# Attention outputs transposed by VectorE in 32x32 blocks, row maxima transposed in a score bank, and LN1 scaled on GpSimd

## The chip, the cores and the metric

The kernel runs on one core of a Trainium2 chip. A core has TensorE (PE, matrix products and transposes into PSUM), VectorE (DVE), ScalarE (ACT), GpSimd (POOL) and SyncE (SP, which issues the DMAs here). The metric is device time in microseconds (us) of one execution; several executions are timed and the median is taken. A trace of one execution shows what each engine did and what each wait ended on.

## The reference

One transformer block with adaptive layer norm: 2048 rows of width 448, 16 heads of width 28, a causal window of 256, and an MLP of width 1792 with the Mish activation.

```python
sa, ca, ga, sb, cb, gb = (silu(c) @ w_mod).reshape(1, 6, 1, -1)[:, i]   # i = 0..5
h = layernorm(x) * (1 + ca) + sa
q, k, v = (h @ wqkv) split into 16 heads of 28
scores = q @ k.T * 28 ** -0.5, masked to 0 <= i - j < 256
x = x + ga * ((softmax(scores) @ v) @ wo)
h = layernorm(x) * (1 + cb) + sb
x = x + gb * (mish(h @ w1 + b1) @ w2)
```

All inputs and the output are float32.

## The kernel before

**Precision.** A float32 product is built from a rounded high part (`float32r`) and the remainder: hi x hi, hi x lo and lo x hi are accumulated in PSUM. `wo` has 448 = 3 x 128 + 64 rows; in the last chunk the 64 rows and their remainders are stacked on 128 partitions, so it takes two products instead of three and an output tile takes 11 products.

**Stages.** The rows are worked in four groups of 512 (`NG`). Per group come LN1 (`gen_ln1`), the transpose of its rows (`gen_hT`), the q, k and v products (`gen_qkv`), the attention of 16 heads, the output product with `wo` (`gen_oT`, `gen_wo`), and LN2. The MLP (`f1_mm`, `ff2`) follows for all groups. The attention of group g is one software pipeline over all 64 heads; the work of the neighbouring groups fills the gaps.

**The pipeline.** A head has three steps; step u = 3s + k belongs to head s and part k. In a step PE does in this order: the product of an earlier step's probability remainders with v (`PV(u-3, Pl)`), the scores of this step (`B`), the scores of a head three ahead for the row maxima (`A`), filler products, one more `A`, and the product of earlier probabilities with v (`PV(u-2, Ph)`). ACT takes the exponential twice (`P` in float32, `Ph` rounded), POOL subtracts them (`Pl`, in `SP(u)`), DVE adds the mask to the scores of `A` and takes the row maximum (`junk`, `mx`). `M2` turns the maxima of two heads with one PE transpose; DVE splits the result into two parts (`mr`) and a DMA writes them into two extra rows of q, so that the scores of `B` come out with the maximum subtracted.

**The attention output.** `PV` accumulates a head in one PSUM bank `pv` as 60 rows: 28 rows from the high part of v, row 28 the sum of the probabilities, three zero rows, and 28 rows from the remainder of v. `EV` copies it to SBUF (ACT; DVE for the last three heads), two heads to a tile `O2`. `E` turns the two heads with four PE transposes of 124 columns into the bank `tr`; `E2` (ACT) copies the remainder rows out of it, `E3` takes the reciprocal of the sums and adds the two parts (DVE) and scales (POOL) into `on`. When the 16 heads of a group are done, `gen_oT` turns `on` back with 16 PE transposes, and ACT and DVE split it into high part and remainder for `wo`.

**What sets the order.** Every engine works its own instructions in program order, which the loop writes out by hand. Filler work for PE is paid out by a credit per step (`RATE`), side work on the other engines by `side_step`, and DMAs that are not urgent from the list `later`. PSUM has eight banks: `sA` 2, `sB` 2, `mm` 2, `tr` 1, `pv` 1. A tile that is allocated again waits until the readers of the older one are done.

Of the kernel before, what the change touches and what calls it, by code (L numbers as in the profile page):

```python
# [51 lines left out]
def adaln_block(ctx: ExitStack, tc: tile.TileContext, x, wqkv, wo, w1, b1, w2, c, w_mod, out):  # L52
# [104 lines left out]
    mask = kq.tile([128, 384], F32, name="mask")  # L157
# [67 lines left out]
    def gen_ln(tiles, pl, xn_tiles, key, mv=None):  # L225
# [12 lines left out]
        for t in range(4):  # L238
            xn = xs[t]
            DVE.tensor_scalar(xn[:, 0:D], tiles[t], mv[:, t, 0:1], rs[:, t:t + 1],  # L240
                              op0=ALU.subtract, op1=ALU.mult)
            if t:
                dup(xs[t - 1])
            yield xs
# [66 lines left out]
    def tile_mms(p, ps):  # L311
        m = 0
        for n, (a, b) in enumerate(ps):
            PE.matmul(p, b, a, start=(n == 0), stop=(n == 10))  # L314
# [185 lines left out]
    first_tiles([(0, bank("pv", 1, "qk0_0")), (3, bank("tr", 1, "qk0_3"))])  # L500
# [17 lines left out]
    O2 = []  # L518
    for i in range(2):
        t = att.tile([128, GT], F32, name=f"o2_{i}")  # L520
        POOL.memset(t[32:64, :], 0.0)
        O2.append(t)
    wo3 = [mid.tile([128, D], F32R, name=f"wo3_{i}", tag="wo", bufs=7) for i in range(4)]
    wol = [mid.tile([128, D], F32R, name=f"wol_{i}", tag="wo", bufs=7) for i in range(3)]
# [5 lines left out]
    def stg(pl, name):  # L530
        return pl.tile([128, 512], F32, name=name, tag="stg", bufs=4)
# [19 lines left out]
    def gen_mod_wo():  # L551
# [14 lines left out]
        for ci in range(4):  # L566
# [5 lines left out]
            split_lo(w, wo3[ci], wol[min(ci, 2)], ci, DVE)  # L572
# [40 lines left out]
    def gen_oT(g, tag, bufs, oT_pool):  # L613
        o = on[g]
        oh, ol = OT[g] = new_T(f"o{g}", oT_pool)

        def oT_out(p, ci):
            DVE.tensor_tensor(ol[:, ci], p, oh[:, ci].bitcast(F32), op=ALU.subtract)

        for ci in range(4):  # L620
            p = bank(tag, bufs, f"ot{g}{ci}")
            tr_chunk([o[:, t] for t in range(4)], ci, p)
            ACT.activation(oh[:, ci], p, AF.Copy)
            pipe.add(1, lambda p=p, ci=ci: oT_out(p, ci))
# [3 lines left out]
            if g == NG - 1:  # L628
                yield
# [6 lines left out]
    def gen_wo(g, tag, bufs):  # L636
# [14 lines left out]
        for t in range(4):  # L651
# [16 lines left out]
    mx, Pt, Ph, Pl, pvb, et, olt = {}, {}, {}, {}, {}, {}, {}  # L668
    junk = att.tile([128, 384], F32, name="junk")

    def A(i, t):
# [5 lines left out]
        p = bank("sA", 2, f"sA{i}_{t}")  # L677
        PE.matmul(p[:, c0:384], q[0:84, t * 128:(t + 1) * 128], k[0:84, t * 128 + c0:t * 128 + 384],  # L678
# [5 lines left out]
    def M2(pr):  # L684
        p = bank("tr", 1, f"mt{pr}")
# [57 lines left out]
    def EV(i):  # L743
        o = O2[i // 2 % 2][64 * (i % 2):64 * (i % 2) + 60]
        if i < NS - 3:
            ACT.activation(o, pvb[i][0:60, :], AF.Copy)  # L746
        else:
            DVE.tensor_copy(o, pvb[i][0:60, :])  # L748

    def E(pr):  # L750
        g, h = divmod(2 * pr, H)
        p = bank("tr", 1, f"et{pr}")
        for t in range(4):
            PE.transpose(p[:, t * 128:t * 128 + 124], O2[pr % 2][0:124, t * 128:(t + 1) * 128], ident[0:124, 0:124])  # L754
        et[pr] = p.rearrange("p (t a d) -> p t a d", t=4, a=2)

    def E2(pr):
        olt[pr] = att.tile([128, 4, 2, 28], F32, name=f"ol{pr}", tag="ol", bufs=2)
        ACT.activation(olt[pr], et[pr][:, :, :, 32:60], AF.Copy)
# [420 lines left out]
```

## Time and profile before

| what | value |
|---|---|
| three runs, median (lowest to highest) | 718.11 us (716.7 to 719.73) |
| profiled execution | 719.96 us |
| span from its first to its last instruction | 718.2 us |
| mean granted TensorE clock | 0.99 |
| attention pipeline | about 50 to 420 us of the span |
| MLP | about 420 us to the end |

The span is cut out of the profiled execution, which has 1.8 us around it. An engine's busy time is the union of its instructions; on PE, products overlap one another, so the distance between starts tells what one costs when PE is full, and not its duration.

### The profile page before, as it was taken

The page shows a single profiled execution, that of the slowest core. Times are in us where ns is not written, and L with a number is a line of the kernel's source. Part 1 is how long each engine was busy: PE and PEld are TensorE (multiplying, and loading weights), DVE is VectorE, ACT ScalarE, POOL GpSimd, SP SyncE. Part 2 cuts the span into 40 slices and gives each one's busy share as a digit, 9 for nine tenths or more (in the row PEclk, how much of TensorE's full clock was granted, in tenths as well). Part 3 has the DMA queues.
Part 4 walks back from the last instruction along what each step waited for, and adds up shares of the span by engine and source line. Part 5 has one row for each costly group of instructions (what it writes and reads, how often), then busy time and mean ns, then how long its engine had stood idle before and what let it go on. Part 6 is the DMA issues. An engine that isn't in the chain of part 4 may idle for free.

```text
span 718.2 us, 12057 instructions
## 1 busy us (share of the span) xinstructions
PE 694.9 (97%) x4049; PEld 597.3 (83%) x4049; DVE 380.0 (53%) x1018; ACT 390.9 (54%) x740; POOL 327.0 (46%) x358
## 2 busy tenths in 40 slices
PE   8999999999999999999999899999999999999996
PEld 8777878788898888898887688888888888888885
DVE  5688657788555878656768642434323232322112
ACT  4538778768766768767868774243224222422221
POOL 6636778676666767666869744422010000000002
PEclk9999999999999999999999899999999999999999
DMA  7865763453761653744672165400200020001001
GB/s 215 257 211 178 251 204 122 148 158 125 212 207 50 203 166 88 230 137 137 216 223 75 52 216 157 116 1 2 102 1 1 4 99 1 0 7 45 0 1 51
DMA packets 48249, 83.86 MB, mean 117 GB/s; under 512 B 6142, under 2 KB 26348, under 8 KB 48188
## 3 DMA queue, kind: packets, MB, share of 16 engines
q1 hardware_dynamic: 47724, 83.10, 37.1%
q8 instruction: 32, 0.52, 0.3%
q14 instruction: 29, 0.24, 0.1%
q10 hardware_dynamic: 464, 0.00, 0.0%
HBM read 53.45 MB, written 29.36 MB: 115 GB/s over the span
## 4 chain that ended last, share of the span: by engine, by line
PE 72%; issue 11%; DVE 8%; DMA 4%; ACT 2%; POOL 1%; SPq 1%; POOLq 0%; DVEq 0%; ACTq 0%
PE z L915 15%; PE pv L740 9%; PE qk L314 8%; PE sA L678 5%; PE acc L1098 5%; PE acc L1100 5%; PE acc L1099 5%; PE sB L708 5%; PE wo L314 4%; PE qk_v L314 4%; PE sB L719 3%; DVE junk L680 3%; PE et L754 2%; DMA q<-mr 1%; DMA scr<-st 1%
## 5 line engine op out<-in xcount | busy, mean ns | idle before, releaser
L730 POOL TENSOR_TENSOR Pl<-P,Ph 128x512 fp32r<-128x512 f32 (+2 forms) x192 | 234.5, 1229 | 87.1 <-ACT Ph L723 49.4
L680 DVE CUSTOM_DVE_ANT_0 junk<-sA,mask 128x384 f32<-128x384 f32 (+2 forms) x256 | 135.2, 528 | 97.8 <-PE sA L678 89.5
L722 ACT ACTIVATE P<-sB 128x512 f32<-128x512 f32 (+2 forms) x192 | 109.8, 572 | 66.9 <-PE sB L719 61.7
L923 DVE TENSOR_TENSOR al<-t,ah 128x512 fp32r<-128x512 f32 x56 | 38.7, 692 | 199.7 <-ACT ah L922 199.7
L921 ACT ACTIVATE t<-z,b1c 128x512 f32<-128x512 f32 x56 | 38.5, 688 | 188.8 <-PE z L915 181.6
L723 ACT ACTIVATE Ph<-sB 128x512 fp32r<-128x512 f32 (+2 forms) x192 | 109.2, 569 | 0.0
L678 PE MATMUL sA<-k,q 84*128 84x384 f32 (+2 forms) x256 | 100.9, 396 | 2.2 <-DVE mx L680 1.5
L915 PE MATMUL z<-hhf,w 128*128 128x512 f32 x224 | 89.6, 400 | 0.0
L915 PE MATMUL z<-hlf,w 128*128 128x512 f32 x224 | 88.4, 395 | 0.0
L1098 PE MATMUL acc<-w2h,ah 128*128 128x448 f32 x224 | 82.0, 366 | 0.0
L1100 PE MATMUL acc<-w2h,al 128*128 128x448 f32 x224 | 81.7, 365 | 0.0
L1099 PE MATMUL acc<-w2l,ah 128*128 128x448 f32 x224 | 81.4, 364 | 0.0
L740 PE MATMUL pv<-Ph,v 128*60 128x256 f32 (+2 forms) x352 | 77.6, 295 | 3.6 <-DVE o L748 2.3
L740 PE MATMUL pv<-Pl,v 128*60 128x256 f32 (+2 forms) x352 | 74.4, 286 | 2.3 <-POOL Pl L730 2.3
L708 PE MATMUL sB<-q,k 86*128 86x256 f32 (+1 forms) x352 | 74.7, 286 | 1.4 <-DMA q<-mr 1.4
L915 PE MATMUL z<-hhf,w1l 128*128 128x512 f32 x168 | 66.3, 395 | 0.0
L708 PEld LDWEIGHTS sB<-q,k 86*128 86x128 f32 x352 | 62.4, 191 | 2.9 <-issue 1.2
L740 PEld LDWEIGHTS pv<-Ph,v 128*60 128x60 f32 x352 | 46.0, 135 | 18.0 <-ACT o L746 3.2
L719 PE MATMUL sB<-fdmask,identr 128*128 128x128 bf16 (+1 forms) x320 | 60.6, 255 | 0.0
L678 PEld LDWEIGHTS sA<-k,q 84*128 84x128 f32 x256 | 48.9, 192 | 8.5 <-DVE mx L680 5.9
L740 PEld LDWEIGHTS pv<-Pl,v 128*60 128x60 f32 x352 | 45.7, 133 | 11.0 <-POOL Pl L730 3.9
L1107 POOL TENSOR_TENSOR yo<-yo,x 128x448 f32<-128x448 f32 (+1 forms) x4 | 4.2, 1064 | 108.1 <-DVE yo L1104 108.1
(156 smaller groups left out, 1300.4 us busy)
## 6 DMA issues: line engine op xcount, KB each, us to landing
scr<-st SPq DMA_DIRECT2D x24, 512.0 KB
k<-scr SPq DMA_DIRECT2D x48, 252.0 KB
q<-scr SPq DMA_DIRECT2D x64, 168.0 KB
scr<-st SPq DMA_DIRECT2D x32, 256.0 KB
x<-x1d SPq DMA_DIRECT2D x10, 448.0 KB
xin<-in_A_x_dram SPq DMA_DIRECT2D x8, 448.0 KB
xr<-in_A_x_dram SPq DMA_DIRECT2D x16, 224.0 KB
x1d<-xr SPq DMA_DIRECT2D x16, 224.0 KB
```

Source lines behind the costliest of these rows:

```text
L314: PE.matmul(p, b, a, start=(n == 0), stop=(n == 10))
L678: PE.matmul(p[:, c0:384], q[0:84, t * 128:(t + 1) * 128], k[0:84, t * 128 + c0:t * 128 + 384], start=True, stop=True)
L680: DVE.tensor_tensor_reduce(out=junk[:, c0:384], in0=p[:, c0:384], in1=mask[:, c0:384], scale=1.0, scalar=-3.0e38, op0=ALU.add, op1=ALU.max ...
L708: PE.matmul(p[:, c:c + 128 * (t1 - t0)], k[:, jj * 128:(jj + 1) * 128], q[:, t0 * 128:t1 * 128], start=(n == 0), stop=False, skip_group_ch ...
L722: ACT.activation(P[:, c0:], p[:, c0:], AF.Exp, scale=SCALE)
L723: ACT.activation(Ph[u][:, c0:], p[:, c0:], AF.Exp, scale=SCALE)
L730: eng.tensor_tensor(Pl[u][:, a:b], Pt[u][:, a:b], Ph[u][:, a:b].bitcast(F32), op=ALU.subtract)
L740: PE.matmul(pv[0:60, t0 * 128:t1 * 128], V[j % NV][:, h, :], P[u][:, c:c + 128 * (t1 - t0)], start=(P is Ph and b == 0 and n == 0), stop=F ...
L915: PE.matmul(zb[n], ps[m][1], ps[m][0], start=(m == 0), stop=(m == 10))
L1098: PE.matmul(p, ah[n][:, ts], w2h[f], start=(f == 0), stop=False)
L1099: PE.matmul(p, ah[n][:, ts], w2l[f], start=False, stop=False)
L1100: PE.matmul(p, al[n][:, ts], w2h[f], start=False, stop=(f == NF - 1))
```

## The change

- **Heads stacked.** `EV` copies the 32 high rows of a head to `O4` and the 28 remainder rows to `OL4`, at partitions 0, 32, 64 or 96, so that four heads (a quad) fill 128 partitions. The two copies are placed in later steps than the one copy before, and `pv` now has two banks.
- **Add, transpose, scale, transpose.** For each quad POOL adds `O4` and `OL4` into `on` (`QA`), DVE transposes it in 32x32 blocks into `T4` and takes the reciprocals of the sums (`T1`), POOL scales (`TM`), and DVE transposes back in blocks (`T2`). In the last quad `QA` and `TM` are shared between POOL and DVE. `E`, `E2`, `E3` and the transposes of `gen_oT` go.
- **wo in 32-row blocks.** The heads now lie 32 partitions apart, so `wo` is loaded as 16 pieces of 28 rows into zeroed tiles, its remainder has four tiles, and an output tile takes 12 products.
- **Maxima.** `M2` writes its transpose into columns 384 to 511 of the older of the two score banks `sA`; in the loop it stands behind the filler products of the step instead of ahead of them. The bank `tr` goes.
- **LN1.** The rows of LN1 of groups 1 to 3 are scaled by POOL instead of DVE. The mask and `junk` are bf16.

```diff
-            DVE.tensor_scalar(xn[:, 0:D], tiles[t], mv[:, t, 0:1], rs[:, t:t + 1],
-                              op0=ALU.subtract, op1=ALU.mult)
+            (POOL if key[0] == "a" else DVE).tensor_scalar(xn[:, 0:D], tiles[t], mv[:, t, 0:1], rs[:, t:t + 1],
+                                                           op0=ALU.subtract, op1=ALU.mult)
...
+        def wo_load(ci, t):
+            for a in range(4):
+                r = (4 * ci + a) * DH
+                dma(t[32 * a:32 * a + DH], wo[r:r + DH, :])
...
         for ci in range(4):
-            p = bank(tag, bufs, f"ot{g}{ci}")
-            tr_chunk([o[:, t] for t in range(4)], ci, p)
-            ACT.activation(oh[:, ci], p, AF.Copy)
-            pipe.add(1, lambda p=p, ci=ci: oT_out(p, ci))
+            ACT.activation(oh[:, ci], o[:, ci], AF.Copy)
+            pipe.add(1, lambda ci=ci: DVE.tensor_tensor(ol[:, ci], o[:, ci], oh[:, ci].bitcast(F32), op=ALU.subtract))
...
-    def M2(pr):
-        p = bank("tr", 1, f"mt{pr}")
+    def M2(pr, b="B"):
+        p = last[b][:, 384:512]
...
-            pvb[i] = bank("pv", 1, f"pv{i}")
+            pvb[i] = bank("pv", 2, f"pv{i}")
...
+    def EV(i, part):
+        a = i % 4 * 32
+        if part == 0:
+            ACT.activation(O4[a:a + 32], pvb[i][0:32, :], AF.Copy)
+        elif i < NS - 3:
+            ACT.activation(OL4[a:a + DH], pvb[i][32:60, :], AF.Copy)
         else:
-            DVE.tensor_copy(o, pvb[i][0:60, :])
+            DVE.tensor_copy(OL4[a:a + DH], pvb[i][32:60, :])
+
+    def QA(qd):
+        o, t = quad(qd)
+        for eng, a, b in ((POOL, 0, GT),) if qd < NS // 4 - 1 else ((POOL, 0, 192), (DVE, 192, GT)):
+            eng.tensor_tensor(o[:, a:b], O4[:, a:b], OL4[:, a:b], op=ALU.add)
+
+    def T1(qd):
+        o, t = quad(qd)
+        DVE.transpose(T4, o)
+        rcq[qd] = att.tile([128, 16, 1], F32, name=f"rc{qd}", tag="rc", bufs=1)
+        DVE.reciprocal(rcq[qd], t[:, :, 28:29])
+
+    def TM(qd):
+        o, t = quad(qd)
+        for eng, a, b in ((POOL, 0, 16),) if qd < NS // 4 - 1 else ((POOL, 0, 6), (DVE, 6, 16)):
+            eng.tensor_tensor(t[:, a:b, 0:28], t[:, a:b, 0:28], rcq[qd][:, a:b].to_broadcast([128, b - a, 28]), op=ALU.mult)
+
+    def T2(qd):
+        o, t = quad(qd)
+        DVE.transpose(o, T4)
...
+            if k == 2 and s % 4 != 1:
+                EV(s - 1, 0)
+        if k == 0 and 0 <= s - 2 < NS:
+            if s % 4 == 2:
+                EV(s - 2, 0)
+            EV(s - 2, 1)
+        qd = (s - 5) // 4
+        if k == 1 and s % 4 == 1 and 0 <= qd < NS // 4:
+            QA(qd)
...
-        if k == 0 and (a - 1) % 2 == 1 and LEAD <= a - 1 < NS:
-            M2((a - 1) // 2)
...
+        if k == 2 and s % 4 == 1 and 0 <= qd < NS // 4:
+            T1(qd)
+            TM(qd)
+        qd = (s - 6) // 4
+        if k == (1 if u < NU else 0) and s % 4 == 2 and 0 <= qd < NS // 4:
+            T2(qd)
...
             while credit > 0.0:
                 credit -= step(g)
+        if k == 0 and (a - 1) % 2 == 1 and LEAD <= a - 1 < NS:
+            M2((a - 1) // 2)
```

The order of instructions on PE around the transpose of the maxima in the second group, before (`sA` the scores for the maxima, `mt` the transposed maxima, `qk` a filler product, `pv` the attention output; `x4` stands for four alike):

```order
L678 MATMUL sA_0_2905<-k_0_141,q_0_376 128x384
L686 MATMUL mt_2908<-ident,mx_2723 8x128
L314 MATMUL qk_4_2879<-hh_2554,wql 128x512
L314 MATMUL qk_4_2879<-hl_2555,wq_105 128x512
L314 MATMUL qk_4_2879<-hh_2554,wq_105 128x512
L314 MATMUL qk_4_2879<-hh_2554,wql 128x512
L740 MATMUL pv_2887<-Ph_2837,v_167 60x256
```

The same place now, as far as the next scores for the maxima:

```order
L679 MATMUL sA_0_2806<-k_0_141,q_0_376 128x384
L314 MATMUL qk_3_2752<-hl_2524,wq_105 128x512
L314 MATMUL qk_3_2752<-hh_2523,wq_105 128x512
L314 MATMUL qk_3_2752<-hl_2524,wq_105 128x512
L687 MATMUL sA_3_2781<-ident,mx_2628 8x128
L741 MATMUL pv_2788<-Ph_2743,v_167 60x256
L741 MATMUL pv_2788<-Ph_2743,v_170 60x256
L741 MATMUL pv_2788<-Pl_2779,v_167 60x256
L741 MATMUL pv_2788<-Pl_2779,v_170 60x256
L709 MATMUL sB_2824<-q_1_458,k_3_147 128x256 x2
L720 LDWEIGHTS identr
L720 MATMUL sB_2824<-fdmask,identr 128x256
```

The transpose has moved behind the fillers and writes into the bank of `sA_3`; the scores that come next on PE, `sA_1`, take that bank over.

PE at the end of a pair of heads, before (`et` the transposed attention output):

```order
L719 MATMUL sB_2961<-fdmask,identr 128x128
L719 LDWEIGHTS identr
L719 MATMUL sB_2961<-fdmask,identr 128x256
L678 MATMUL sA_3_2972<-k_0_141,q_0_376 128x384
L754 MATMUL et_2975<-ident,o_0_462 128x124 x4
```

None of the rows of `et`, nor of the later `ot`, is left in the changed kernel's order.

POOL in the second group, before, from one scaling of a pair of heads (L770) to the next (`Pl` the subtraction of a step, `xin` the copy of 64 columns behind LN1):

```order
L770 TENSOR_TENSOR on_971<-ol_2080,rc_2106 128x4x56
L772 COPY on_971<-on_971 128x4x64
L730 TENSOR_TENSOR Pl_2139<-P_2097,Ph_2098 128x512
L730 TENSOR_TENSOR Pl_2165<-P_2135,Ph_2136 128x512
L730 TENSOR_TENSOR Pl_2198<-P_2161,Ph_2162 128x512
L730 TENSOR_TENSOR Pl_2231<-P_2194,Ph_2195 128x512
L223 COPY xin_1111<-xin_1111 128x64
L730 TENSOR_TENSOR Pl_2264<-P_2227,Ph_2228 128x512
L223 COPY xin_1111<-xin_1111 128x64
L730 TENSOR_TENSOR Pl_2293<-P_2260,Ph_2261 128x512
L770 TENSOR_TENSOR on_2298<-ol_2271,rc_2299 128x4x56
```

The same stretch now (L240 the rows of LN1, L762 the add `QA`, L775 the scaling `TM`):

```order
L240 TENSOR_SCALAR xin_1100<-xin_1100,mva_1918,rsa_2047 128x448
L223 COPY xin_1100<-xin_1100 128x64
L731 TENSOR_TENSOR Pl_2221<-P_2189,Ph_2190 128x512
L731 TENSOR_TENSOR Pl_2247<-P_2217,Ph_2218 128x512
L240 TENSOR_SCALAR xin_1100<-xin_1100,mva_1918,rsa_2047 128x448
L223 COPY xin_1100<-xin_1100 128x64
L731 TENSOR_TENSOR Pl_2277<-P_2243,Ph_2244 128x512
L223 COPY xin_1100<-xin_1100 128x64
L762 TENSOR_TENSOR on_2300<-o_462,ol_463 128x512
L731 TENSOR_TENSOR Pl_2310<-P_2273,Ph_2274 128x512
L731 TENSOR_TENSOR Pl_2347<-P_2306,Ph_2307 128x512
L775 TENSOR_TENSOR t_464<-t_464,rc_2353 128x16x28
```

POOL now has the rows of LN1 between its subtractions, and the add and the scaling of a quad with two subtractions between them.

More of the change, by code (lines that the diff above doesn't have):

```diff
@@ L516, in adaln_block @@
     k3_tile(att, NK - 1)
[L518 to L524, printed above, removed]
+    O4, OL4, T4 = [att.tile([128, GT], F32, name=n) for n in ("o4", "ol4", "t4")]
+    POOL.memset(OL4, 0.0)
+    wo3 = [mid.tile([128, D], F32R, name=f"wo3_{i}", tag="wo", bufs=8) for i in range(4)]
+    wol = [mid.tile([128, D], F32R, name=f"wol_{i}", tag="wo", bufs=8) for i in range(4)]
     def xr_tile(name):
@@ L571, in gen_mod_wo @@
             yield "dve"
-            split_lo(w, wo3[ci], wol[min(ci, 2)], ci, DVE)
+            split_lo(w, wo3[ci], wol[ci], 0, DVE)
             yield
@@ L1126, in adaln_block @@
     chunk["v"] = 6
-    fill = chain(gen_oT(NG - 1, "tr", 2, ff), gen_wo(NG - 1, "tr", 2), finish(), gen_x1_ln2(1))
+    fill = chain(gen_oT(NG - 1, ff), gen_wo(NG - 1, "tr", 2), finish(), gen_x1_ln2(1))
     def fill_step():
```

82 lines of the change are left out of this document (29 added, 53 removed).

## The prediction

> **What bounds the kernel now.** I read the page's busy times and chain first, then the windows by stage, then what PE waited for.
>
> ```profile
> span 718.2 us, 12057 instructions
> PE 694.9 (97%) x4049; PEld 597.3 (83%) x4049; DVE 380.0 (53%) x1018; ACT 390.9 (54%) x740; POOL 327.0 (46%) x358
> PE 72%; issue 11%; DVE 8%; DMA 4%; ACT 2%; POOL 1%; SPq 1%; POOLq 0%; DVEq 0%; ACTq 0%
> ...
> 60.00:420.00 360.00, 347.99 (x2355) 297.57 (x2354) 251.12 (x768) 266.69 (x533) 255.04 (x240) 0.99 0.51 157
> 480.00:660.00 180.00, 180.00 (x849) 155.64 (x849) 58.11 (x90) 55.28 (x84) 8.52 (x16) 1.00 0.08 26
> 140.00:150.00 10.00, 9.24 (x66) 7.60 (x66) 9.21 (x24) 7.90 (x16) 9.09 (x11) 1.00 0.63 198
> 380.00:400.00 20.00, 17.80 (x134) 14.53 (x133) 17.16 (x50) 16.95 (x33) 19.34 (x20) 1.00 0.19 57
> 400.00:410.00 10.00, 7.08 (x54) 6.12 (x53) 6.52 (x11) 7.21 (x15) 7.09 (x7) 0.87 0.31 93
> ```
>
> In a window row the numbers after the length are PE, weight loads, DVE, ACT and POOL. In the MLP PE has no gap, and the change touches nothing there but the head of it. In the attention (60 to 420 us) PE is busy for 348 of 360 us while ACT has 74%, POOL 71% and DVE 70%: PE sets the pace, yet all three helpers are well loaded. Two places differ. At 140 to 150 us, where LN1 of the next group falls, DVE and POOL are both above 9 of 10. At 380 to 400 us the fillers are used up and POOL, 19.3 of 20, is the bound; after it PE idles by 2.9 of 10 us and its granted clock falls to 0.87.
>
> ```profile
> PEld pv L740 <- POOL Pl L730: 3.9, 6, 0.8
> PEld pv L740 <- ACT o L746: 3.2, 8, 0.9
> PEld pv L740 <- DVE o L748: 2.5, 1, 2.5
> PEld mt L686 <- DVE mx L680: 2.3, 3, 0.9
> ```
>
> The waits (total, times, longest) are small. The first says that a subtraction on POOL was late for PE in 6 of 192 steps only; the next two are the single `pv` bank, the last the maxima.
>
> **PE work.** These rows give the counts, and the chain of waits gives what a run of four costs where PE is full.
>
> ```profile
> L754 PE MATMUL et<-ident,o 124*128 124x124 f32 x128 | 19.3, 273 | 0.0
> L249 PE MATMUL ot<-ident,on 128*128 128x128 f32 x64 | 9.4, 272 | 0.0
> L314 PE MATMUL wo<-wol,hho 128*128 128x448 f32 x48 | 17.8, 371 | 0.0
> ...
> 91.91 0.43 PE et L754 x4
> 96.59 0.82 PE qk_v L314 x4
> 138.29 0.44 PE ot L249 x4
> ```
>
> Gone are 128 / 4 = 32 runs of `et` at 0.43 us, 13.8 us, and 64 / 4 = 16 runs of `ot` at 0.44, 7.0 us. Added are 16 products of 448 columns (`wol` 48 to 64) at 0.82 / 4 = 0.205, 3.3 us. Net **-17.5 us** of PE work, nearly all inside the attention.
>
> **Waits on `pv`.** With two banks and the copies a step later, nothing on PE should wait for them: -3.2 us. At the end the 2.5 us wait for DVE's copy goes too, but PE would soon wait for the last subtractions there; I count half. Together **-4.4 us**, between -5.7 and 0.
>
> **Maxima.** Behind the fillers, `M2` finds its maxima ready: up to -2.3 us. But `sA_1` now takes over its bank and must wait for both `mr` instructions of DVE.
>
> ```profile
> 87.98 0.27 PE L686 MATMUL mt<-ident,mx 128*8 128x128 f32 x1
> 88.71 0.28 DVE L689 TENSOR_TENSOR mr<-mt,mr 8x128 fp32r<-8x128 f32 x1
> 155.14 0.27 PE L686 MATMUL mt<-ident,mx 128*8 128x128 f32 x1
> 156.94 0.28 DVE L689 TENSOR_TENSOR mr<-mt,mr 8x128 fp32r<-8x128 f32 x1
> ...
> 80.52 0.47 PE pv L740 x4
> 80.99 0.24 PE sB L708 x2
> 81.23 0.18 PE sB L719 x2
> ```
>
> From the transpose to the end of `mr` it takes 1.01 us at 88 us and 2.08 us at 155 us, where DVE had other work. PE reaches `sA_1` after 0.11 (a quarter of 0.43) + 0.47 + 0.24 + 0.18 = 1.00 us. So the wait is between 0 and 1.1 us, 32 times: 0 to 35 us. In the old order DVE still had the first scores' maximum to take at that moment; now the fillers' time lets it finish. I take the near end, 0.07 each or 2.3 us, which cancels the gain: **0**.
>
> **ACT.**
>
> ```profile
> L746 ACT ACTIVATE o<-pv 60x512 f32<-60x512 f32 x61 | 36.0, 590 | 23.5 <-PE pv L740 22.9
> L759 ACT ACTIVATE ol<-et 128x224 f32<-128x224 f32 x32 | 11.6, 362 | 0.0
> ```
>
> A copy's time goes by its 512 columns, so 64 + 61 copies at 0.59 = 73.8 replace 36.0 + 11.6: +26 us, 85% of a loop of some 345 us. They lie beside PE's work; without that cover they would cost the 26 us. For steps in which two copies stand ahead of the exponentials I take **+2**.
>
> **POOL.**
>
> ```profile
> L770 POOL TENSOR_TENSOR on<-ol,rc 128x224 f32<-128x224 f32 x32 | 18.0, 564 | 23.5 <-DVE ol L768 11.0 <-ACT Ph L723 10.1 <-PE ot L249 1.5
> L568 POOL TENSOR_TENSOR wop<-wop,ga 128x448 f32<-128x448 f32 x4 | 4.6, 1154 | 0.0
> L160 POOL TENSOR_SCALAR_AFFINE_SELECT mask<-mask 128x384 f32<-128x384 f32 x1 | 0.5, 508 | 0.1
> ...
> L730 POOL TENSOR_TENSOR Pl<-P,Ph x192: 727/1286/1676, 49.1 to 414.2; 128x512 fp32r<-128x512 f32 x155, 128x256 fp32r<-128x256 f32 x21, 128x384 fp32r<-128x384 f32 x16
> ...
> 60.00:420.00 360.00, 2.94 (x5) 226.86 (x184) 0.99 0.51 157
> ```
>
> A quad costs the add, 1.29 (as `Pl` over 512 columns), and the scaling of 448 elements, 1.15 (as `wop`): 2.44 in place of two scalings, 1.13, so +1.3 a quad and +21 us over 16. The 12 rows of LN1 have no row of their own on POOL: below stands the select over 384 columns, 0.51, above the 1.15 of a two-input instruction; with one input they are nearer the first, 0.6 each, +7. POOL goes from 255 to some 280 us of 345, 81%. A step lasts 360 / 184 = 1.96 us (the last row counts the subtractions) against 1.29 for `Pl`, and a remainder is used three steps after its scores, which leaves it about 3.9 - 1.29 = 2.6 us of slack once the exponentials are done. A quad's 1.3 fits into that. Two places do not have it: at 380 to 417 us POOL is the bound, so 1.5 quads cost 2.0 there and the three or four runs of `et` saved there bring nothing, 1.3: **+3.3**. And in the two stretches like 140 to 150 us, 2.4 for LN1 and 1.3 for the quad meet 0.9 us of room. POOL falls behind by 2.8, just past its slack, while DVE is relieved: **+1**.
>
> [...]
>
> **DVE.**
>
> ```profile
> L767 DVE RECIPROCAL rc<-et 128x8 f32<-128x8 f32 x32 | 6.5, 202 | 1.6 <-ACT ol L759 1.6
> L768 DVE TENSOR_TENSOR ol<-ol,et 128x224 f32<-128x224 f32 x32 | 10.7, 335 | 0.0
> L748 DVE COPY o<-pv 60x512 f32<-60x512 f32 x3 | 2.0, 683 | 0.8 <-PE pv L740 0.7
> ...
> L240 DVE TENSOR_SCALAR xin<-xin,mva,rsa x12: 498/854/1504, 41.5 to 256.6; 128x448 f32<-128x448 f32 x12
> L240 DVE TENSOR_SCALAR xn<-x,mv,rsf x12: 499/508/1346, 463.7 to 602.1; 128x448 f32<-128x448 f32 x12
> ...
> L730 DVE TENSOR_TENSOR Pl<-P,Ph x5: 406/424/1015, 407.9 to 414.2; 128x256 fp32r<-128x256 f32 x5
> ```
>
> Gone: 6.5 + 10.7 + 12 x 0.93 = 28. No row shows a block transpose. The lone 448-column pass, 0.51, bounds it below, and the same pass beside a busy POOL, up to 1.50, above; a plain 512-column copy took 0.68, which I take: 32 x 0.68 = 21.8, and 16 reciprocals 3.2. The `hlo` subtractions now read two SBUF tensors; such a one took 0.42 to 1.02 on half the columns, so 12 of them lose perhaps 0.4 each, 5. In all +2 on DVE, hidden in its 30%: **0**. At the upper bound the transposes would add 26 more, 80% of DVE.
>
> [...]
>
> **The sum.** -17.5 - 4.4 + 0 + 2 + 3.3 + 1 + 0 = -15.6, from the profiled 719.96 to 704.4. That execution lies 1.9 us above the median of 718.11; from the median it is 702.5, and I say **703 us**.
>
> **The rivals.**
> - *Everything pays*: the helpers keep up, PE's waits for `pv` and for maxima go entirely, LN1's relief of DVE counts. -17.5 - 5.7 - 2.3 = -25.5: **693**. For it: POOL late only 6 times. Against it: the POOL-bound end.
> - *PE no longer sets the pace*: POOL's add, DVE's transpose and POOL's scaling run one after the other in a quad. In those four steps POOL needs 4 x 1.29 + 2.44 = 7.6 of 7.8 us; if it also waits for DVE's transpose by more than its 2.6 us of slack, PE stops. At 3.5 us a quad loses 0.9, 15 of them 13 us: **716**. For it: DVE passes of up to 1.50 us. Against it: two subtractions stand between add and scaling.
> - *The score bank stalls PE* (slower): each `M2` holds its bank until DVE is through, and `sA_1` stops all of PE behind it. At 0.8 us in each of 32, 26 us: 702.5 + 26 = **728**. It decides from 15.6 / 32 = 0.5 us each, that is when `mr` ends 1.5 us after the transpose. For it: the 2.08 at 155 us. Against it: 1.01 at 88 us, and the fillers' head start.
> - *The change does not do what it says*: the bf16 mask makes each of 256 maxima slower on DVE. Scores still come from PSUM in float32, so I expect no difference; 0.1 us each would be 26 us on DVE, and with that some **712**.
>
> **How the numbers follow.** Chances: forecast 0.55 (697 to 711), everything pays 0.16, pace lost 0.11, score bank 0.14, mask 0.04. The range 690 to 718 takes in the first cases and most of the pace lost. A measurement here can tell 0.5%, 3.6 us, from no change. Faster (under 714.5): 0.55 + 0.16 + 0.04 and a quarter of the pace lost, 0.77. Within: 0.09 from the lost pace and the smaller stalls of the bank. Slower: 0.14.
>
> **What would show it.** `et` and `ot` are gone and PE's busy time is 17 us lower, with its idle time about as before; no `pv <- o` wait; `sA <- DVE` waits under 8 us; block transposes at 0.6 to 0.8 us; ACT near 85%, POOL near 81% of the loop. If PE's idle time between 60 and 400 us grows by over 10 us, the forecast is wrong, and who it waits for names the rival.

## The result, and the profile after

| | before | changed |
|---|---|---|
| median of four runs (lowest to highest) | 717.87 us (716.7 to 719.73) | 728.25 us (728.02 to 728.94) |
| profiled execution, its span | 719.96, 718.2 us | 728.02, 726.2 us |
| mean granted TensorE clock of that execution | 0.990 | 0.979 |

The changed kernel is slower: ratio 1.0144, 95% interval 1.0121 to 1.0167, that is +10.3 us where 15.6 less was forecast. First the page of the changed kernel (span and busy times), which answers to the first lines of the prediction.

```profile
span 726.2 us, 11790 instructions
PE 689.5 (95%) x3873; PEld 586.1 (81%) x3873; DVE 397.5 (55%) x992; ACT 422.5 (58%) x772; POOL 368.9 (51%) x369
```

PE's busy time fell by only 5.4 us, and the span grew by 8.0. The window from the first to the last exponential of the attention shows how. The columns are start and end, length, busy time (and instructions) of PE, weight loads, DVE, ACT and POOL, then the granted clock, the share of the DMA engines and GB/s. Before:

```profile
48.12:413.06 364.94, 352.19 (x2396) 300.82 (x2395) 255.84 (x789) 271.33 (x547) 260.60 (x246) 0.99 0.52 160
```

The changed kernel, the same stretch and three of the windows that the prediction showed:

```profile
47.51:423.59 376.08, 350.30 (x2243) 293.31 (x2242) 268.06 (x765) 303.40 (x580) 295.76 (x258) 0.96 0.50 155
...
140.00:150.00 10.00, 6.30 (x39) 4.07 (x37) 9.08 (x23) 9.83 (x19) 9.92 (x8) 0.96 0.61 191
380.00:400.00 20.00, 17.73 (x124) 14.92 (x122) 17.50 (x47) 18.05 (x34) 17.30 (x16) 1.00 0.45 132
400.00:410.00 10.00, 9.06 (x49) 7.70 (x50) 7.47 (x22) 6.52 (x13) 7.41 (x9) 0.66 0.02 4
```

The stretch is 11.1 us longer, and the rest of the span 3.1 us shorter. PE's idle time in the stretch went from 364.94 - 352.19 = 12.75 us to 376.08 - 350.30 = 25.78: +13.0. Between 60 and 400 us, where the prediction put its sign of being wrong, it went from 9.1 to 21.4 us, past the 10 us named there. And PE's busy time fell by 1.9 us though it has 153 records less; most of the difference is the clock, 0.96 against 0.99, as worked out below. From 140 to 150 us, where LN1 falls, PE is busy for 6.3 us in place of 9.2.

The waits between 45 and 420 us of the changed kernel (in all, how often, the longest), PE's and one of DVE's:

```profile
PE pv L741 <- POOL Pl L731: 12.0, 15, 1.9
PE sA L679 <- DVE mx L681: 5.2, 8, 1.5
PE sA L679 <- DVE mr L690: 2.0, 1, 2.0
...
DVE mr L689 <- PE sA L687: 9.7, 20, 1.2
```

Before, the first two were 2.3 and 1.5 us, and DVE waited 0.4 us for the turned maxima. PE's waits for `o` are gone, as forecast. In the groups by operation and shape (busy time, mean ns, idle time before) the new work reads:

```profile
L747 ACT ACTIVATE o<-pv 32x512 f32<-32x512 f32 x64 | 37.3, 583 | 22.8 <-PE pv L741 22.4
L749 ACT ACTIVATE ol<-pv 28x512 f32<-28x512 f32 x61 | 35.9, 589 | 1.3
L240 POOL TENSOR_SCALAR xin<-xin,mva,rsa 128x448 f32<-128x448 f32 x12 | 23.2, 1936 | 0.1
L762 POOL TENSOR_TENSOR on<-o,ol 128x512 f32<-128x512 f32 x15 | 19.2, 1283 | 0.7 <-DVE hlo L622 0.7
L622 DVE TENSOR_TENSOR hlo<-on,hho 128x512 fp32r<-128x512 f32 x16 | 18.6, 1175 | 1.8 <-ACT hho L621 1.5
L775 POOL TENSOR_TENSOR t<-t,rc 128x448 f32<-128x448 f32 x15 | 14.4, 962 | 13.1 <-DVE rc L770 9.5 <-PE sB L720 1.9 <-PE qk L314 1.4
L768 DVE STREAM_TRANSPOSE t<-on 128x512 f32<-128x512 f32 x16 | 11.3, 706 | 0.1
```

Most durations are as forecast: copies 0.59, transposes 0.71 (0.68), add and scaling together 2.25 us a quad (2.44). One is not: an LN1 row takes 1.94 us on POOL, where 0.6 was taken. The timeline of POOL, and two rows of PE with the idle time ahead of them and what ended it, show what that does.

```profile
141.86 4.63 POOL L731 TENSOR_TENSOR Pl<-P,Ph 128x512 fp32r<-128x512 f32 x3
146.48 2.35 POOL L240 TENSOR_SCALAR xin<-xin,mva,rsa 128x448 f32<-128x448 f32 x1
148.81 2.49 POOL L731 TENSOR_TENSOR Pl<-P,Ph 128x512 fp32r<-128x512 f32 x2
151.30 1.85 POOL L240 TENSOR_SCALAR xin<-xin,mva,rsa 128x448 f32<-128x448 f32 x1
...
150.12 0.68 PE L741 MATMUL pv<-Pl,v 128*60 128x128 f32 x2 [1.82 <-POOL Pl L731]
...
248.05 0.61 PE L741 MATMUL pv<-Pl,v 128*60 128x128 f32 x2 [1.14 <-POOL Pl L731]
```

The row of LN1 stands ahead of two subtractions in POOL's queue; `Pl` comes 2.35 us later, and PE stands still for 1.82 us. It then pays a second time. Windows of the same execution, cut at the change of the clock:

```profile
146.00:149.40 3.40, 2.24 (x13) 1.42 (x13) 3.12 (x10) 3.35 (x7) 3.40 (x3) 0.97 0.20 46
149.40:156.20 6.80, 6.08 (x23) 5.31 (x24) 1.14 (x4) 2.90 (x6) 6.80 (x6) 0.51 0.87 277
156.20:160.00 3.80, 3.80 (x28) 3.40 (x27) 2.42 (x7) 2.71 (x6) 3.80 (x5) 1.00 0.12 35
...
248.40:251.80 3.40, 3.40 (x17) 3.00 (x17) 3.36 (x9) 2.95 (x7) 3.40 (x3) 0.53 0.69 210
255.10:258.50 3.40, 3.40 (x13) 3.02 (x14) 0.56 (x2) 1.51 (x3) 3.40 (x4) 0.51 0.97 355
360.90:367.70 6.80, 6.60 (x26) 5.76 (x27) 4.78 (x15) 4.69 (x9) 5.34 (x5) 0.51 0.50 161
401.70:408.50 6.80, 6.47 (x31) 5.42 (x29) 5.20 (x15) 5.07 (x9) 5.13 (x8) 0.50 0.02 4
```

After such pauses PE ran at half its clock (0.50 to 0.53 granted) for 3.4 or 6.8 us while it nearly always had work; in the rows at 149.4 and 255.1 us DVE and ACT mostly stood idle behind it. The half-clock rows hold 6.8 + 3.4 + 3.4 + 6.8 + 6.8 = 27.2 us at about 0.5, which cost 13.6 us of PE's full-speed time. Before, there were 6.8 us of it, at the end of the attention:

```profile
407.80:414.60 6.80, 6.65 (x32) 6.04 (x33) 3.00 (x7) 3.71 (x8) 3.16 (x4) 0.52 0.00 1
```

So the account of the attention's +11.1 us is: PE's work about -13.0 (worked out below), half clock +13.6 - 3.4 = +10.2, idle time +13.0, and 0.9 not placed. Not every pause brought it: one of 1.14 us that ended at 143.18 us did not. Those ahead of the five rows at half clock belong to three edits: LN1 rows at 148 to 150, 247 and 254 us, the `hlo` subtractions at 357 to 361, the maxima at 399.

### The profile page after: what moved, and what is told of

Read it like the earlier page. It is cut to its first block, busy times and chain, and to the rows that moved or that the text cites. A ratio compares the mean times of both kernels' runs of the same rounds, so it can differ in the third digit from the quotient of the medians.

```text
span 726.2 us, 11790 instructions
## 1 busy us (share of the span) xinstructions
PE 689.5 (95%) x3873; PEld 586.1 (81%) x3873; DVE 397.5 (55%) x992; ACT 422.5 (58%) x772; POOL 368.9 (51%) x369
## 5 line engine op out<-in xcount | busy, mean ns | idle before, releaser
L681 DVE CUSTOM_DVE_ANT_0 junk<-sA,mask 128x384 bf16<-128x384 f32 (+2 forms) x256 | 134.4, 525 | 93.6 <-PE sA L679 84.6
L931 DVE TENSOR_TENSOR al<-t,ah 128x512 fp32r<-128x512 f32 x56 | 40.7, 726 | 188.3 <-ACT ah L930 188.3
L679 PE MATMUL sA<-k,q 84*128 84x384 f32 (+2 forms) x256 | 103.9, 408 | 8.2 <-DVE mx L681 5.2
L741 PE MATMUL pv<-Pl,v 128*60 128x256 f32 (+2 forms) x352 | 76.7, 293 | 12.8 <-POOL Pl L731 12.0
L741 PE MATMUL pv<-Ph,v 128*60 128x256 f32 (+2 forms) x352 | 79.2, 300 | 0.0
L709 PE MATMUL sB<-q,k 86*128 86x256 f32 (+1 forms) x352 | 76.8, 293 | 2.1 <-ACT Ph L724 1.4
L679 PEld LDWEIGHTS sA<-k,q 84*128 84x128 f32 x256 | 50.8, 200 | 15.5 <-DVE mx L681 9.2
```

The costliest lines, as they stand in the source:

```text
L681: DVE.tensor_tensor_reduce(out=junk[:, c0:384], in0=p[:, c0:384], in1=mask[:, c0:384], scale=1.0, scalar=-3.0e38, op0=ALU.add, op1=ALU.max ...
L709: PE.matmul(p[:, c:c + 128 * (t1 - t0)], k[:, jj * 128:(jj + 1) * 128], q[:, t0 * 128:t1 * 128], start=(n == 0), stop=False, skip_group_ch ...
L741: PE.matmul(pv[0:60, t0 * 128:t1 * 128], V[j % NV][:, h, :], P[u][:, c:c + 128 * (t1 - t0)], start=(P is Ph and b == 0 and n == 0), stop=F ...
```

## The experiments

Steps are given by the ratios to the kernel before, of which 0.1% is 0.72 us. By the two intervals a step between two runs has a margin of some 1.6 to 2.6 us; that of e13 against e12 has 3.9. "Clock lost" is (1 - granted clock) times span, the median over all executions of a kernel; the kernel before has 3.6 us of it and the changed one 15.3.

| run | median us | ratio [95%] | clock lost, us |
|---|---|---|---|
| changed kernel | 728.25 | 1.0144 [1.0121, 1.0167] | 15.3 |
| e1_ln1_dve | 724.94 | 1.0097 [1.0075, 1.0118] | 10.5 |
| e2_ln1_pool_alone | 721.49 | 1.0057 [1.0039, 1.0075] | 2.9 |
| e3_m2_bank_alone | 721.74 | 1.0054 [1.0038, 1.0070] | 2.2 |
| e4_ln1_dve_lo_later | 721.18 | 1.0046 [1.0029, 1.0064] | 6.5 |
| e5_add_on_dve | 736.66 | 1.0265 [1.0242, 1.0287] | 9.5 |
| e6_no_add_no_scale | 718.59 | 1.0014 [1.0000, 1.0027] | 5.4 |
| e7_add_on_dve_ln1_act | 732.87 | 1.0202 [1.0189, 1.0215] | 11.7 |
| e8_m2_front | 720.40 | 1.0028 [1.0016, 1.0041] | 7.2 |
| e9_no_block_work | 714.80 | 0.9955 [0.9938, 0.9973] | 5.7 |
| e10_ln1_act_lo_pool | 729.20 | 1.0164 [1.0143, 1.0185] | 6.6 |
| e11_before_more_dve | 720.03 | 1.0027 [1.0013, 1.0041] | 3.6 |
| e12_before_no_turn | 709.28 | 0.9872 [0.9844, 0.9901] | 4.6 |
| e13_no_turn_act_copy | 710.65 | 0.9900 [0.9854, 0.9946] | 7.1 |
| e14_no_turn_m2_bank | 713.93 | 0.9933 [0.9913, 0.9954] | 7.8 |
| e16_turn_beside_qkv | 720.83 | 1.0035 [1.0019, 1.0050] | 8.6 |
| e17_m2_pv_bank | 725.16 | 1.0091 [1.0070, 1.0113] | 7.6 |
| e18_m2_pv_bank_front | 745.93 | 1.0369 [1.0334, 1.0403] | 14.5 |
| e19_no_turn_m2_later | 712.14 | 0.9927 [0.9906, 0.9948] | 6.4 |

**LN1's rows.** e1 is the changed kernel with them back on DVE; e2 the kernel before with nothing changed but them.

```diff
-            (POOL if key[0] == "a" else DVE).tensor_scalar(
+            DVE.tensor_scalar(
```

> The changed kernel with the LN1 rows scaled by DVE again, all else kept. Theory 'LN1 rows on POOL': in the changed kernel each of the 12 rows takes 1.86 us on POOL, PE waits 3.4 us for late subtractions in each of the stretches 140-151 and 245-256 us (0.7 before), and the granted clock then falls to 0.5-0.9 for 15 us, some 3.3 us more each time. Without it the two stretches give back 2 x (2.7 + 3.3) = 12 us: about 716 us, no clock below 0.95 at 145-160 and 245-260 us. Rival 'score bank': the maxima's transposes set the loss, so the time stays at 725 us or more. Rival 'a quad's add, transposes and scaling set the pace': 723 us or more, with POOL's subtractions still late everywhere.

> The kernel before, with one part of the change alone: the LN1 rows scaled by POOL. Theory 'LN1 rows on POOL': the same stall and the same fall of the clock in two stretches, +8 to +12 us, so 726 to 730 us. Rivals 'score bank' and 'quads': LN1 is harmless, 716 to 721 us.

e1 takes off 0.47%, 3.4 us, and 4.8 us of lost clock; e2 adds 0.57%, 4.1 us. Both ways the edit costs 3 to 4 us, about a third of what I had expected; e1's time lies where its rivals put it. e2 and e3 (below) cost theirs without more half clock than before has, by waits alone (PE's waits for `Pl` go from 2.3 to 7.0 us in e2); in the changed kernel LN1's rows also bring half clock. The group rows of e2 confirm the duration without the rest of the change beside it:

```profile
L240 POOL TENSOR_SCALAR xin<-xin,mva,rsa 128x448 f32<-128x448 f32 x12 | 22.4, 1864 | 0.1
```

**The remainder of the attention output (`hlo`).** e4 is e1 with this subtraction one step later, so that DVE no longer reaches it before ACT's `hho` is there.

```diff
-            pipe.add(1, lambda ci=ci: DVE.tensor_tensor(ol[:, ci], o[:, ci], oh[:, ci].bitcast(F32), op=ALU.subtract))
+            pipe.add(2, None, lambda ci=ci: DVE.tensor_tensor(ol[:, ci], o[:, ci], oh[:, ci].bitcast(F32), op=ALU.subtract))
```

> As e1_ln1_dve, and the remainder of the attention output (hlo) is taken on DVE one step later, so that DVE does not stand waiting for ACT's high part. Theory 'a late DVE stops PE': in the changed kernel DVE waits 1.17 and 0.35 us for ACT at 356-359 us, the subtraction then takes 1.4 us beside POOL, PE stands 1.47 and 0.92 us at its scores and the clock falls; without the wait 2 to 5 us less than e1. Rival: the long subtraction itself, and not the wait ahead of it, is the cause: no more than 1 us less than e1.

It takes off 0.51%, 3.7 us, and 4.0 us of lost clock. DVE waited for `hho` only twice, 1.5 us in all, but one of these held a score's maximum behind it. The mean `hlo` also became shorter, 1.31 us in e1 and 1.10 in e4, so e4 does not tell the wait from the length. Nor does it bring back the `hlo` of the kernel before, which read one input from PSUM and took 0.69 us each time; with both in SBUF the longest of e4 takes 1.76 us, at 248.04, and PE then waits 1.54 us for a maximum. The timeline of the changed kernel, DVE and then PE:

```profile
356.92 1.41 DVE L622 TENSOR_TENSOR hlo<-on,hho 128x512 fp32r<-128x512 f32 x1 [1.17 <-ACT hho L621]
358.25 0.55 DVE L681 CUSTOM_DVE_ANT_0 junk<-sA,mask 128x384 bf16<-128x384 f32 x1
...
358.86 0.44 PE L679 MATMUL sA<-k,q 84*128 84x384 f32 x1 [1.47 <-DVE mx L681]
```

e10 puts LN1's rows on ACT and `hlo` on POOL, with the rest as in e4.

```diff
-            pipe.add(2, None, lambda ci=ci: DVE.tensor_tensor(ol[:, ci], o[:, ci], oh[:, ci].bitcast(F32), op=ALU.subtract))
+            pipe.add(2, None, lambda ci=ci: POOL.tensor_tensor(ol[:, ci], o[:, ci], oh[:, ci].bitcast(F32), op=ALU.subtract))
...
+            if key[0] == "a":
+                ACT.activation(xn[:, 0:D], tiles[t], AF.Identity, scale=rs[:, t:t + 1], bias=nm[:, t:t + 1])
```

> e4_ln1_dve_lo_later (721.2 us) with the LN1 rows on ACT and the remainder of the attention output on POOL: DVE loses 11 + 18 us, ACT gets 7, POOL 20. Theory 'DVE is the second bound': 709 to 716 us, below the kernel before. Rival 'all helpers are alike': 719 us or more.

It is 1.2% slower than e4, for both moves together: 21.3 us more for POOL, and PE's wait for `Pl` goes from 9.3 to 15.7 us (PE's waits of e10):

```profile
PE pv L747 <- POOL Pl L737: 15.7, 22, 1.7
```

**The work on the quads.** e6 is e4 without the add and the scaling on POOL: the transpose reads `O4`, the remainder of v is not added and nothing is divided by the sums. e9 leaves out the transposes and reciprocals as well; the output product gets zeros.

```diff
-        if k == 1 and s % 4 == 1 and 0 <= qd < NS // 4:
-            QA(qd)
...
-            TM(qd)
```

```diff
-            T1(qd)
...
-        DVE.transpose(o, T4)
```

> e4_ln1_dve_lo_later (721.2 us) without POOL's two instructions of a quad: the block transposes read the high part directly, the remainder part is copied but not added, and nothing is scaled, so the attention output lacks both. POOL has 35 us less. Theory 'POOL is the second bound: late subtractions give back what PE saved': PE's waits for Pl (9.3 us, and many below 0.25 us) fall to a third, 707 to 713 us. Rival 'DVE, late at its maxima, gives it back': no more than 3 us less, 718 us or more.

> e6_no_add_no_scale (718.6 us) without the block transposes and reciprocals too: the heads are copied out of PSUM and dropped, and the output product takes a zeroed tile. PE's work is that of the changed kernel; DVE has 27 us less than in e6. Theory 'DVE is the second bound: its late maxima stop PE at the score banks, at about 0.35 us for each us of DVE work (e5 and e7)': 707 to 711 us, with PE's waits for DVE's maxima at most half of e6's. Rival 'what remains is elsewhere (ACT's second copy, the score bank, the place of the fillers)': 715 us or more.

POOL's 34 us are worth 0.32%, 2.3 us; DVE's 23 us of transposes and the reciprocals 0.59%, 4.2 us. PE's waits, two of e6 and one of e9:

```profile
PE sA L679 <- DVE mx L681: 6.4, 14, 1.3
PE pv L741 <- POOL Pl L731: 3.5, 7, 0.9
...
PE sA L680 <- DVE mx L682: 3.1, 6, 0.8
```

The wait for `Pl` was 9.3 us in e4, so the quads do make the subtractions late, and most of that between 45 and 380 us (6.8 us in e4, 2.4 in e6); the wait for maxima halves when the transposes go too. And without any of it the kernel is 3.2 us faster than before, not 15: most of the miss lies elsewhere.

**More work for DVE.** In e5 (from e4) DVE adds the remainder rows straight from PSUM, so ACT has no second copy and POOL no add, and the first transpose of a quad comes one step earlier; e7 is e5 with LN1's rows on ACT; e11 is the kernel before with 32 transposes of a constant.

```diff
-            ACT.activation(OL4[a:a + DH], pvb[i][32:60, :], AF.Copy)
+            DVE.tensor_tensor(O4[a:a + DH], pvb[i][32:60, :], O4[a:a + DH], op=ALU.add)
```

```diff
+        if 0 <= (s - 5) // 4 < NS // 4 and ((k == 2 and s % 4 == 1) or (k == 1 and s % 4 == 2)):
+            DVE.transpose(junk, mask)
```

> e4_ln1_dve_lo_later, but DVE adds the remainder rows straight from PSUM onto the copied high rows, so ACT's second copy (36 us) and POOL's add (20 us) go and DVE gets 64 additions of some 0.69 us (44 us). Theory 'POOL is the second bound': 711 to 717 us. Rival 'DVE gives it back': the time rises, 722 to 735 us, with PE waiting for maxima.

> e5_add_on_dve with the LN1 rows of groups 1 to 3 scaled by ACT, which has room there: DVE loses 12 x 0.9 us. If DVE limits e5, 2 to 6 us less than e5; if not, within 2 us of it. If POOL was the second bound of the changed kernel, this one is below the kernel before: 708 to 716 us.

> The kernel before with two block transposes of 128x384 from the mask into DVE's scratch tile for each four heads, where the changed kernel has its own: 32 x 0.57 = 18 us of DVE work that nothing waits for, about what DVE gained in e4_ln1_dve_lo_later. Theory 'DVE is the second bound': 722 to 726 us. Rival 'DVE has 30% to spare': 717 to 720 us.

e5 is 2.2% slower than e4, past even the rival's 722 to 735 us. Its groups and PE's waits:

```profile
L748 DVE TENSOR_TENSOR o<-pv,o 28x512 f32<-28x512 f32 x64 | 43.8, 684 | 7.3 <-ACT o L746 5.5
...
PE sA L678 <- DVE mx L680: 21.1, 33, 1.7
```

DVE's 43.8 us, ahead of which it waits 5.5 us more for ACT with the maxima standing behind, turn into 21.1 us of waits on PE (4.7 in e4). e7 gets 0.63 of the 2.2% back. In e11 18.4 us more cost 1.9 us: a tenth, where they wait for nobody.

**PE's saving by itself.** e12 is the kernel before without the turning: no `et`, no `E2` and `E3`, no `ot`. The outputs are neither turned nor normalised, and the output product gets zeros. Its `hlo` is in the later place as in e4 and, as in the changed kernel, reads two SBUF tiles. e13 adds a second copy on ACT per head, e14 the changed kernel's `M2`.

```diff
-            p = bank(tag, bufs, f"ot{g}{ci}")
-            tr_chunk([o[:, t] for t in range(4)], ci, p)
-            ACT.activation(oh[:, ci], p, AF.Copy)
+            ACT.activation(oh[:, ci], ONZ[:, ci], AF.Copy)
...
-                E(pr)
...
-            (E2, E3)[k]((s - 4) // 2)
```

```diff
+        if k == 0 and 0 <= s - 2 < NS - 3:
+            i = s - 2
+            ACT.activation(OX[0:28], O2[i // 2 % 2][64 * (i % 2):64 * (i % 2) + 28], AF.Copy)
```

> The kernel before without the work of turning: no et transposes, no copies, adds and scalings behind them, no ot transposes; gen_oT reads a zeroed tile, so the outputs are not normalised or turned and the output product gets zeros. pv, EV, the maxima and wo are as before. From start to start the four et take 0.35 us and the four ot 0.355, so PE has 32 x 0.35 + 16 x 0.355 = 16.9 us less. Theory 1 (PE sets the pace and the changed kernel lost its gain to its own new work): 718 - 17 = 701, at most 703. Theory 2 (the helpers and their waits stand just behind PE all along, so that PE's saving is only partly passed on even with less work on every other engine): 706 to 711, with PE's idle time in the attention larger by 5 to 9 us.

> The same kernel without the work of turning, and for 61 of the 64 heads ACT copies 28 rows of 512 a second time, from SBUF to a tile that nothing reads, at the step in which the changed kernel takes its second copy: 61 x 0.59 = 36 us more on ACT and nothing else. Theory 1 (ACT has room, the prediction's +2 for 26 us): at most 2 us above e12. Theory 2 (a copy ahead of the exponentials makes P and Ph late for PE): 4 to 7 us above e12, with a wait of sB or pv for ACT in PE's list.

> The same kernel without the work of turning, with the maxima turned in the older score bank behind the fillers. Theory 1 (the move of the maxima costs nothing, as predicted): 0 to 1 us above e12. Theory 2 (the later maxima and the shared score bank cost the same 3.6 us as they did alone, or more now that PE has less work to hide them): 3 to 6 us above e12, with sA waiting for DVE's mr or for the row of q.

e12 takes off 9.2 us of the 16.9 that PE no longer works. The window from its first to its last exponential and PE's waits, which answer to the row before:

```profile
48.61:403.69 355.08, 335.07 (x2226) 281.64 (x2224) 249.06 (x728) 263.75 (x517) 247.27 (x212) 1.00 0.54 164
...
PE sA L677 <- DVE mx L679: 6.2, 11, 1.5
PE pv L739 <- ACT o L745: 3.4, 6, 1.2
```

PE's busy time falls by 17.1, but its idle time grows from 12.75 to 20.0, though DVE, ACT and POOL all have less to do in sum. So the time and the growth of idle time are the second theory's: part of what PE saves it then waits, for maxima above all (1.5 us before) and for ACT's copy out of `pv` (1.2 before). But the helpers did not all stand where they stood before: of the 6.2 us two waits of 1.54 come right behind two long `hlo`, of 1.76 and 1.77 us, where the kernel before has 0.69. DVE and then PE of e12, the first of the two:

```profile
142.69 1.76 DVE L619 TENSOR_TENSOR hlo<-onz,hho 128x512 fp32r<-128x512 f32 x1
144.38 0.54 DVE L679 CUSTOM_DVE_ANT_0 junk<-sA,mask 128x384 f32<-128x384 f32 x1
...
144.99 0.44 PE L677 MATMUL sA<-k,q 84*128 84x384 f32 x1 [1.54 <-DVE mx L679]
```

So 3.1 of the 7.3 us of added idle time stand behind the new form of `hlo`, and not behind work that was there before; no run has the turning gone and `hlo` reading PSUM. e13 costs 2.0 us, but its interval overlaps that of e12, so anything from nothing to some 6 us fits. e14 costs 4.4, against the prediction's 0, and its lost clock is 3.2 us higher than e12's.

**The maxima.** e3 is the kernel before with the changed `M2` alone; e8 is e4 with `M2` ahead of the fillers again, still in the score bank. e17 turns the maxima, behind the fillers, in the `pv` bank that has just been copied out; e18 does it a step later, ahead of the fillers; both are built on e4. e19 is e12 with `M2` in its own bank `tr`, but behind the fillers.

```diff
             while credit > 0.0:
                 credit -= step(g)
+        if k == 0 and (a - 1) % 2 == 1 and LEAD <= a - 1 < NS:
+            M2((a - 1) // 2)
```

> The kernel before, with one part alone: the maxima transposed in the older score bank, behind the fillers. Theory 'LN1 rows on POOL': PE's waits for mr are small (2.0 us in the whole changed kernel), so 715 to 721 us. Rival 'score bank': 0.8 us in each of 32, 728 us or more.

> e4_ln1_dve_lo_later with the maxima's transpose ahead of the fillers again, still in the older score bank. If the bank's takeover by the next scores costs PE anything, it now costs less, since the fillers lie between: 717 to 720 us. If the place behind the fillers was the better one, as the wait for the maxima says, 721 to 724 us.

> The kernel e4 (LN1 on DVE, the hi/lo subtraction one step later) with the maxima turned in the pv bank of the head that has just been copied out, still behind the fillers, so that no score bank is held. If the shared score bank is what made the move cost 4.6 us beside e12: about 717 against e4's 721.2. If it is the later place behind the fillers: 721.

> As e17, with the transpose of the maxima one step later and ahead of its fillers (its row of q is then due four rather than six microseconds after it). If what counts is the wait of PE's next scores for the bank: as e17, 717. If it is the lateness of the row of q: slower than e17, 720 or more, with sB waiting for the DMA of the row.

> The kernel e12 (without the work of turning) with the maxima still turned in a bank of their own, but behind the filler products as in the changed kernel. If the shared score bank makes the 4.6 us of e14 against e12: 709 to 710.5. If it is the later place (mr and the row of q come later, and DVE takes them among other work): 713 to 714.5.

e3 costs 3.9 us. e19, with the place alone, costs 3.9 by the ratio and 2.9 by the medians, where e14, with place and bank, costs 4.4 and 4.65; its interval (0.9906 to 0.9948) overlaps that of e14 and not that of e12. So in this kernel the place is most of it, though 712.14 falls between the two times expected. The bank's own wait, PE for `mr`, is 1.3 us in e3 and in e14, and not there in e19. DVE's waits of e19 show what the place changes:

```profile
DVE mr L687 <- PE mt L685: 8.1, 21, 0.9
```

The same wait is 0.4 us in e12 and in the kernel before, 9.7 in the changed kernel. `mr` stands at its turn on DVE while PE still works the fillers, and the next scores' maxima stand behind it. How much of that reaches PE is less clear: its wait for maxima goes from 1.5 to 3.6 us in e3, and only from 6.2 to 7.6 in e19. In e8 DVE's wait is gone, yet only 0.18%, 1.3 us, is won, less than the margin; its trace has more of other waits (`Pl` 10.7 us, 9.3 in e4; `M2` for its maxima 1.7, 0.7 in e4) and none for `mr`. So what the maxima cost inside the changed kernel isn't measured; no run there gives them their own bank and their old place. e17 and e18 are misses that tell of other things: PE's wait in e17, and the longest one in e18:

```profile
PE pv L687 <- ACT ol L749: 9.9, 10, 2.4
```

```profile
PE sB L709 <- DMA q<-mr: 14.8, 12, 2.6
```

e17's bank is not yet copied out when PE comes to it, so it says nothing about the score bank. In e18 the row of q comes too late by its DMA, and the time is 745.93 us.

**Steps without filler products.** e16 is e8 with `gen_oT`'s steps, which hold no PE work any more, taken together with the last q and k products.

```diff
-            yield from gen_oT(g - 1, mid)
+                o = "END" if oT is None else next(oT, "END")
+                w = next(q6, "END")
```

> The kernel e8 with gen_oT's four steps, which hold no PE work any more, taken in the same steps as the last q and k products of the group (groups 1 and 2) and not in steps of their own. If steps without filler products are what keeps PE idle near 175 and 275 us, the two groups gain about 1 to 2 us together: 718.5 to 719.5 against 720.4. If the helpers bound those stretches however the products are dealt out: 720 to 721.

720.83 against 720.40: no gain. How the fillers are dealt out there isn't the cause.

No version of the change that computes the whole output beats the kernel before; the nearest is e8, at 1.0028.

## Why the prediction was wrong

The removals form a chain from the changed kernel down to e9, and the additions one from e12 up. Their steps by ratio: -9.2 (no turning) + 2.0 (ACT's copy) + 4.4 (maxima) = -2.8. e9, which has the extra `wol` products and the second `pv` bank too, measures -3.2, which leaves -0.4 for these and everything else that the two chains don't share; that is within the margins of the steps. Then + 4.2 (transposes) + 2.3 (add and scaling) + 3.7 (`hlo`) + 3.4 (LN1) = +10.4, against +10.3 measured. The second chain closes by construction, as each of its steps is the difference of two neighbours, so the sum is no test of it; and each part was taken out in one order only.

| step of the prediction | forecast | measured |
|---|---|---|
| the turning on PE | -13.8 - 7.0 = -20.8 | -9.2 |
| `wol` products and waits on `pv` | +3.3 - 4.4 = -1.1 | -0.4, a remainder |
| maxima | 0 | +4.4 |
| ACT's copies | +2 | +2.0 |
| POOL's quads, the end included | +3.3 | +2.3 |
| LN1's rows | +1 | +3.4 |
| DVE's transposes and `hlo` | 0 | +4.2 + 3.7 = +7.9 |

The rows match only roughly: the forecasts for ACT, POOL and DVE are net of the old turning's work on them, which e12 takes out in its -9.2, and e12 also has the slower `hlo`.

- **"Gone are 32 runs of `et` at 0.43 us"** failed first, in size. The chain's 0.43 runs to the end of the last product of a run; the next instruction starts earlier. The timeline of the kernel before, in its full stretches:

```profile
196.07 0.42 PE L678 MATMUL sA<-k,q 84*128 84x384 f32 x1
196.33 0.59 PE L754 MATMUL et<-ident,o 124*128 124x124 f32 x4
196.67 0.48 PE L740 MATMUL pv<-Ph,v 128*60 128x128 f32 x2
```

From start to start a run takes 196.67 - 196.33 = 0.34; the median over the runs is 0.35, and 0.355 for `ot`. So PE saves 32 x 0.35 + 16 x 0.355 - 3.3 = 13.6, not 17.5; in the stretch of the exponentials, where 12 of the 16 `ot` and of the added products lie, 11.2 + 4.3 - 2.5 = 13.0.
- **"PE sets the pace"** failed in kind, and is the largest miss: of the 16.9 us that e12 takes off PE, 9.2 reach the time. It was read from shares, PE 97% and the helpers 70 to 74%, and from four waits called small; the longest of PE's rows in that view of the kernel before is not among them:

```profile
PEld sA L678 <- DVE mx L680: 5.9, 17, 0.6
```

17 times PE's weight load for the next scores waited for DVE's maximum, so DVE stood right behind PE already. In e12 PE waits for single results of the helpers whose sums leave room: 3.1 us behind the longer `hlo`, the rest spread over maxima, ACT's copies and others.
- **"the copies a step later"** with two banks, for -4.4 us: the waits for `o` went, as forecast, but PE's idle time did not fall with them. The first copy stands in the same step as before for three heads in four; the second, and the first of every fourth head, come a step later.
- **"A lone 0.51 below, 1.15 above, with one input nearer the first, 0.6"** failed: 1.86 alone and 1.94 in the change, above both bounds. That one input puts it near the lower row was the author's estimate; no run shows 0.6 for this operation with two per-partition scalars, and the 12 rows took 22.4 us on POOL in e2 where the forecast had 7 (DVE took 0.83 each in e4).
- **Maxima, "0"**, asked whether PE waits for DVE's `mr`. It does so once, for 2.0 us. The wait went the other way: DVE waits for PE behind the fillers.
- **DVE, "hidden in its 30%"** had the mean durations nearly right (0.706 for 0.68, 1.18 for about 1.1 of `hlo`) and the cover wrong. An instruction that DVE works ahead of a maximum can delay PE although DVE has time to spare: in e12, with DVE busy for 249.06 of 355.08 us, PE waited 1.54 us behind an `hlo` of 1.76; in e11 18.4 us of such work cost 1.9, in e9 against e6 some 27 us cost 4.2.
- **Half clock after pauses** was in no term, though the prediction quoted the 0.87 after the idle POOL-bound end. It is 15.3 - 3.6 = 11.7 us of PE's time over all executions, spread over the steps above: the removals of LN1 and `hlo` took off 4.8 and 4.0.
- **What held:** the vanished waits for `o`, the durations of copies, transposes and quads, and the bf16 mask (a maximum over 384 columns took 550 ns, 553 before). ACT's copies agree with +2 only within a margin that takes in 0 as well. The quads' 2.3 us are near the forecast by luck: it had them free in the loop, inside 2.6 us of slack, and paid at the end, but PE's waits for `Pl` that go with them in e6 lie mostly ahead of 380 us.

Of the rivals, the score bank's 728 is the time that came, but not its mechanism: `sA` waited for `mr` once. "PE no longer sets the pace" names the right kind, at 716, with the quads as the cause; the quads were 2.3 us of it. What stays open is how the 4.4 us of the maxima divide between place and bank, what e12 would be with the old `hlo`, and its other waits one by one: taking work off each helper in turn there wasn't tried.

## What to carry to other kernels

Here one engine was at 97% and its helpers at 70 to 74%, and of the 16.9 us of start-to-start time that e12 took off that engine 9.2 were passed on; what follows was set by waits for single results, not by shares. Before work is moved to a helper, look at what stands behind it in that queue and whether its own input may be late: DVE's wait of 1.17 us for `hho` reached PE as one of 1.47. And a pause of PE of 1 to 2 us may have to be priced twice, with the pause and with the half clock after it: 6.8 us at 0.51 came after 1.82 us.

## What the runs showed of the hardware

- In the changed kernel half clock lasted 3.4 us from 248.4 us (0.53 granted), with a pause of 1.14 us that ended at 248.05 us, and 6.8 us from 149.4 us (0.51), with one of 1.82 us that ended at 150.12 us, while a pause of 1.14 us that ended at 143.18 us was followed by none. PE was busy for 1.84 us of the 3.4 ahead of the stretch at 248.4 us, for 2.24 of those ahead of 149.4 us, and for 2.46 of those from 142.6 to 146.0 us, after which the clock was at 1.00 up to 149 us. In all e18 lost 14.5 us of clock.
- A scaling of 448 columns by two per-partition scalars took 1.86 (e2) to 1.94 us (changed kernel) on POOL and 0.51 on DVE in the MLP of the kernel before (median of 12), while the two-input subtraction of 512 columns on POOL took 1.32 us (`Pl`, changed kernel).
- DVE's `hlo` with both inputs in SBUF took 0.69 us at 148.2 us and 1.41 at 356.92 in the same execution, and from 0.68 to 1.77 in e12; with one input in PSUM, in the kernel before, all 16 took 0.68 to 0.69. On POOL (e10) it took 1.34.
- The `Pl` subtractions of 512 columns took 1.32 us with the block transposes beside them in the changed kernel and 1.31 without (e9), so the transposes' cost is not a slower POOL.
